# Second expert layer, phase 2: the transposes of a pair of token tiles rank ahead of the products of the pair before

## The chip, the core and the metric

The kernel runs on one core of one Trainium2 chip. The metric is the time of one execution on the device in microseconds (us), the median over several runs. The engines are PE (TensorE: matrix products and transposes), ACT (ScalarE), DVE (VectorE), POOL (GpSimd) and SP (SyncE, which here issues the DMAs). Each has its own stream of instructions and executes it in order; between engines there are semaphores.

## The reference

The reference has three stages, all in fp32. Attention with softmax over 4 batches, 12 heads, 448 positions and 64 channels, with a mixing of the heads before and after the softmax, gives 1792 tokens of 768 channels. A first expert layer takes them through a 2048 wide layer and a gate. The second expert layer, which the change touches, is

```
h    = x @ w_in                                   # 1792 x 1024
e    = exp(h - max(h));  sm = e / (sum(e) + 1e-9)
solu = h * sm
mu   = mean(solu);  var = mean((solu - mu)**2)
ln   = (solu - mu) / sqrt(var + 1e-6) * g_ln
out  = ln @ w_out                                 # 1792 x 768
```

## The kernel before

The second expert layer has two phases. Phase 1 computes h, phase 2 computes ln @ w_out. Each works on 7 pairs of 128-token tiles (14 tiles, numbered 0 to 13; pair p holds tiles 2p and 2p+1). A pair's matrix product is a 2 by 2 block product done in seven block products instead of eight; so a pair has seven *products*, numbered 0 to 6. In what follows [p,i] is product i of pair p in phase 2. A product of phase 2 is one call of `wide_mm` with 12 matmuls (L1184 to L1186, 128x384 each): four slices of the inner length, and for each the three partial products of values split into a high and a low part. A product of phase 1 is 9 matmuls of 128x512 on the same lines. g_ln is multiplied into the weights beforehand.

For phase 2 a tile goes through this chain. After phase 1 its exponentials, and for tiles 6 to 13 its h too, were written to DRAM. `el_load` (L1101) issues from SP the loads that bring them back: `el` are the exponentials, `hl` is h, 512 KB each. For pairs 3 to 6 there follows the chain `solu`: a sum and a reciprocal of small columns, `h2_solu` (L1145, DVE), `h2_mean` (L1150, POOL), `h2_square` (L1153, ACT), `h2_rstd` (L1156 to L1158, POOL). For pairs 0 to 2 that was done in phase 1. Then `el_ln` (L1169, ACT) normalises the tile in place, and `tr` (L1106, PE) transposes it: two calls per tile, i = 0 and 1, each four 128x128 transposes into one of 4 PSUM banks of the ring `pstr`. I write tr[t,i] for such a call. Of the transposed blocks, ACT makes plain copies (`lf_copy`, L1113), DVE sums of blocks (`l_sum`, L1119), and of each block or sum ACT makes the high part (`l_h`, L1130) and DVE the low part (`l_l`, L1133). These are the left operands of the products. A product accumulates in a PSUM bank; `part_copy` (L1201, ACT) and `part_add` (L1204, DVE) fold the banks into the output tile, and SP stores it (L1264).

The order of all this is written by a planner, the class `Order` (L69 to L191), while the kernel is built. Each task has an engine, a planned duration, a priority (a lower number goes first), the tasks that it needs, and places in rings of buffers. The planner plays the time through: on the engine that comes free first it takes, among the tasks that are ready by then in its plan, the one with the lowest priority number. What comes out is one fixed stream per engine; on the chip, an instruction waits for its semaphores at the head of its stream and holds up all behind it. The pairs' priorities are 20 apart: `make_front(p, q0)` makes the front of pair p (loads, solu, normalising, transposes) with numbers counted from q0, which is the number at which that pair's seven products start (q0 to q0 + 0.6). So the products of the pair before start at q0 - 20.

Of the kernel before, what the change touches and what calls it, by code (L numbers as in the profile page):

```python
# [68 lines left out]
class Order:  # L69
# [12 lines left out]
    def add(self, eng, dur, prio, fn, *a, deps=(), new=(), join=(), use=(), lat=None):  # L82
        dur = int(dur * SCALE.get(fn.__name__, 1))
        t = Task(eng, dur, (fn, a), prio, deps, lat)
        self.tasks.append(t)
        for r in new:
            r.first.append([t])
            r.users.append([t])
        for r in join:
            r.first[-1].append(t)  # L90
            r.users[-1].append(t)
        for r, k in use:
            r.users[k].append(t)
        return t
# [563 lines left out]
def moe(nc, od, pl, c1, c2, last_x, r_sr, r_psa, r_psb, near, xs, c_near, c_in2, c_out2, c_t1, c_t2, c_o2, xe2, xh2, w_in, w_out, w_in2, w_out2, g_ln, ident_in, out):  # L658
    add = od.add
# [3 lines left out]
    ring = {n: od.ring(b) for n, b in dict(raw=2, m=2, v=1, win=3, wout=3, xl=2, g=4, t=2, st2=3).items()}  # L663
# [220 lines left out]
    for s in range(NS):  # L884
# [20 lines left out]
        if 0 < s < NS - 1:  # L905
            for q in range(min(len(todo), 4 if s < 3 else 3)):
                e, pr = todo.pop(0), base - 6 + 10 * q
                if isinstance(e, tuple):
                    kk, i = e
# [4 lines left out]
        for ch in range(4):  # L914
# [3 lines left out]
            for i, j in enumerate(js):  # L918
                step, a = 1 if u < 2 else 6, None
                for k0 in range(0, 6, step):  # L920
                    a = add("PE", 567 * step, pr + i, h_mm, u, j, xk, k0, step, deps=[a] if a else wd['in', j] + xd[ch],
                            use=[(ring['win'], j), xi[ch]],
                            **(dict(join=[ring['psh']]) if a else dict(new=[ring['psh']])))
# [7 lines left out]
            for m in range(6):  # L931
                a = add("PE", 1134, pr + 14 + 0.1 * m, o_mm, u, js, m, deps=gs + wd['out', js[0]] + wd['out', js[1]] + [o2],
                        new=[ring['pso2']],
                        use=[(ring['wout'], js[0]), (ring['wout'], js[1]), (ring['g'], 2 * u), (ring['g'], 2 * u + 1)])
                b = add(*(("Activation", 424) if s == 0 else ("DVE", 531)), pr + (14 if u < 30 else -25) + 0.1 * m, o_add, u, s, ch, m,
                        deps=[a] + acc_d.get((ch, m), []), use=[(ring['pso2'], -1)])
# [52 lines left out]
    for k in range(3):  # L989
        for c in range(2):  # L990
            pr = 1285 + 2 * k + c
            r = (ring['raw'], len(ring['raw'].users))
            a = od.dma("SP", 900, 1500, pr - 8, prep1_load, k, c, new=[ring['raw']],
                       deps=[o1] + ([ready2[k + 3 * i, h] for i in range(2) for h in range(2)] if wide else []))
            a = add("DVE", 4 * 330, pr, prep1, k, c, deps=[a], use=[r])
# [65 lines left out]
    for i, (_, _, b) in enumerate(SEVEN):  # L1061
        for k in range(3):
            q, r = divmod(3 * i + k, 5)
            rg = ('sr', 'sr', 'xl', 'xl', 'w1x')[q]
            if b[0] == 'T':
                src, deps = c_t1[:, k, TI[b]], [t1_d[k, c] for c in range(2)]
            else:
                kk, h = k + 3 * (int(b[0]) - 1), int(b[1]) - 1
                src, deps = src_in2[:, kk, 512 * h:512 * h + 512], ([ready2[kk, h]] if wide else [])
# [90 lines left out]
    def solu(t, pr, deps, ue, uh):  # L1160
        x = add("Pool", 250, pr, h2_guard, t, deps=deps)
        x = add("DVE", 163, pr, h2_recip, t, deps=[x])
        y = add("DVE", 1360, pr, h2_solu, t, deps=[x], use=uh + ue)
        x = add("Pool", 250, pr, h2_mean, t, deps=[y])
        x = add("Activation", 1330, pr, h2_square, t, deps=[x], use=uh + ue)
        return y, add("Pool", 1300, pr, h2_rstd, t, deps=[x])
# [101 lines left out]
    for k in range(4):  # L1268
        pr = PR + 10 + 20 * k
        at, bs = len(ring['ot'].users), []  # L1270
        for i in range(2):
            a = od.dma("SP", 450, 1130, pr - 8, prep2_load, k, i, new=[ring['ot']], deps=[ch_, o2] + ([ready2[k + 4 * i]] if wide else []))
            a = add("Activation", 734, pr, prep2_gain, k, i, deps=[a], use=[(ring['ot'], -1)])
            t2_d[k, i, 0] = od.dma("SP", 450, 1130, pr, prep2_keep, k, i, deps=[a], use=[(ring['ot'], -1)])
            bs += [a, t2_d[k, i, 0]]
        a = add("Pool", 4 * 930, pr, prep2, k, deps=bs, use=[(ring['ot'], at), (ring['ot'], at + 1)])
# [7 lines left out]
    def make_front(p, q0):  # L1284
        for a in range(2):
            t = 2 * p + a
            rg = ring['h2' if p < EARLY else 'wout']
            ue, uh = [(rg, len(rg.users))], [(ring['h2'], len(ring['h2'].users))]
            x = od.dma("SP", 450, 1500, q0 - 25, el_load, t, 0, deps=[ln_d[t]], new=[rg])
            if p >= EARLY:  # L1290
                y = od.dma("SP", 450, 1500, q0 - 25, el_load, t, 1, deps=[lh_d[t]], new=[ring['h2']])
                _, x = solu(t, q0 - 11, [x, y, ls_d[t]], ue, uh)
            x = add("Activation", 1240, q0 - 11, el_ln, t, deps=[x, ls_d[t]], use=ue)
            for i in range(2):
                m = add("PE", 436, q0 - 12 + 0.1 * (2 * a + i), tr, t, i, deps=[x], new=[ring['pstr']], use=ue)
                front[t, i] = m, [(ring['pstr'], len(ring['pstr'].users) - 1)]

    for p in range(7):
        pr = PR + 20 * p
        if p == 6:  # L1300
            make_front(0, PR + 112)
# [4 lines left out]
        for dst, a, b, op_ in (('S1', '21', '22', ALU.add), ('S2', 'S1', '11', ALU.subtract), ('S3', '11', '21', ALU.subtract), ('S4', '12', 'S2', ALU.subtract)):  # L1306
# [3 lines left out]
                          use=[(ring['s'], si[q]) for q in (a, b) if q in si and q != dst])  # L1310
        ld = []
        for i, (_, q, _) in enumerate(SEVEN):
            us = [(ring['s'], si[q])] if q in si else []
            x = add("Activation", 500, px + 0.1 * i, x2_h, p, i, q, deps=[sm[q]] if q in sm else ad, use=us, new=[r_x2[i]])
# [6 lines left out]
        for a, (own, ds) in enumerate(seven(0, p, pr, ld, [sum((w1_d[i, k] for k in range(3)), []) for i in range(7)], r_x2)):  # L1321
            t = 2 * p + a
# [3 lines left out]
            ue = [(ring['wout'], -1)]  # L1326
# [19 lines left out]
    for p in range(7):  # L1346
        pr = PR + 300 + 20 * p
        if p:
            make_front(p, pr)
        lc, prev, q0 = {}, [], pr - (0, 168)[p == 0]  # L1350
        for a in range(2):
            for i in range(2):
                t = 2 * p + a
                q = '%d%d' % (a + 1, i + 1)
                m, up = front[t, i]
# [10 lines left out]
        for i, (_, q, _) in enumerate(SEVEN):  # L1366
# [7 lines left out]
            x = add("Activation", 595, q0 - 9 + 0.1 * i, l_h, p, i, q, use=us, new=[rl], deps=dep + before)  # L1374
            y = add("DVE", 675, q0 - 9 + 0.1 * i, l_l, p, i, q, deps=[x], use=us + [(rl, -1)])
            ld.append([x, y])
        for a, (own, ds) in enumerate(seven(1, p, pr, ld, [sum((w2_d[i, k] for k in range(4)), []) for i in range(7)], r_lt[p % 2])):
            t = 2 * p + a
# [83 lines left out]
```

## Time and profile before

| quantity | value |
|---|---|
| time, median of 3 runs | 1074.84 us (1074.3 to 1077.52) |
| time of the profiled execution | 1078.25 us |
| its span in the profile | 1076.4 us |
| mean granted TensorE clock over the span | 0.987 |
| PE busy | 1026.5 us, 95% of the span |
| DVE, ACT, POOL busy | 69%, 58%, 33% of the span |

The span is the time from the first to the last instruction that the profiler recorded; the execution's time holds 1.85 us more. PE is busy nearly throughout, so the time of the kernel is the PE's work plus what PE waits and what it loses to a lower clock. The granted clock is a share of full speed: 1.00 is the level of 2.4 GHz, and one half is the level of 1.2 GHz. Phase 2's products of pairs 1 to 6 run from 970 us on and end at 1073 us.

### The profile page before, as it was taken

What the parts mean: (1) busy time and instruction counts of PE and PEld (TensorE: products, weight loads), DVE (VectorE), ACT (ScalarE), POOL (GpSimd) and SP (SyncE); (2) the same over time, 40 slices, a digit from 0 to 9 for tenths busy, and PEclk for the clock granted to TensorE, in tenths of its full rate; (3) what the DMA queues carried; (4) which work ended last, traced back from release to release, by engine and by line L of the source; (5) the groups of instructions that cost most, each with busy time, mean ns of one, the idle gap of its engine ahead of it and who ended that gap; (6) DMA issues with size and microseconds to landing.
All of it is one profiled execution on the core that took longest, in us unless ns stands there. A gap on an engine that the chain in (4) does not pass through costs nothing.

```text
span 1076.4 us, 27349 instructions
## 1 busy us (share of the span) xinstructions
PE 1026.5 (95%) x11053; PEld 840.0 (78%) x11053; DVE 741.8 (69%) x1259; ACT 621.6 (58%) x1329; POOL 352.5 (33%) x475
## 2 busy tenths in 40 slices
PE   7779988999999899999999999999999999989998
PEld 2436555665666589999999999999999888889997
DVE  4445654555555863488898668898876999867674
ACT  3666967778878665533344344343435577767562
POOL 3111321211111341445555455554611244052110
PEclk9899999999999999999999999999999999998999
DMA  8766787478575560242424233423274556695321
GB/s 170 201 174 167 209 251 200 139 213 227 170 222 189 176 201 1 83 135 85 148 69 138 88 118 98 152 89 132 96 227 155 198 210 232 226 355 177 106 84 59
DMA packets 101422, 171.41 MB, mean 159 GB/s; under 512 B 22752, under 2 KB 77888, under 8 KB 101296
## 3 DMA queue, kind: packets, MB, share of 16 engines
q1 hardware_dynamic: 100560, 168.46, 50.3%
q0 software_dynamic: 736, 1.21, 0.6%
q8 instruction: 87, 1.43, 0.6%
q14 instruction: 39, 0.32, 0.1%
HBM read 91.07 MB, written 39.85 MB: 122 GB/s over the span
## 4 chain that ended last, share of the span: by engine, by line
PE 77%; DMA 11%; DVE 5%; ACT 4%; issue 2%; POOL 1%; SPq 1%; ACTq 0%; DVEq 0%
PE ps_h L820 7%; PE ps_o L850 7%; PE ps_h L822 7%; PE ps_o L852 7%; PE ps_h L821 7%; PE ps_o L851 7%; DMA sr<-s 5%; PE ps_pre L340 5%; PE ps_av L427 5%; PE ps_post L376 4%; PE ps_qk L313 4%; PE ps_h L1184 3%; PE ps_h L1186 3%; PE ps_h L1185 3%; PE ps_ot L1186 3%; PE ps_ot L1184 3%
## 5 line engine op out<-in xcount | busy, mean ns | idle before, releaser
L345 DVE TENSOR_REDUCE nm<-ps_pre 128x1 f32<-128x448 f32 x180 | 105.8, 618 | 54.1 <-PE ps_pre L340 45.0
L850 PE MATMUL ps_o<-g,wout 128*128 128x448 f32 x384 | 139.4, 363 | 0.3 <-DVE x2acc L860 0.3
L852 PE MATMUL ps_o<-g,wout 128*128 128x448 f32 x384 | 139.2, 363 | 0.0
L851 PE MATMUL ps_o<-g,wout 128*128 128x448 f32 x384 | 138.3, 360 | 0.0
L376 PEld LDWEIGHTS ps_post<-wr,p 64*64 64x64 f32 x5040 | 103.1, 135 | 43.9 <-issue 28.5
L350 ACT ACTIVATE p<-ps_pre,nm 128x448 f32<-128x448 f32 x180 | 114.1, 642 | 23.6 <-DVE nm L345 22.9
L313 PE MATMUL ps_qk<-kraw,qb 64*64 64x448 f32 (+2 forms) x768 | 110.2, 593 | 12.5 <-DMA qb<-in_q_dram 5.1
L842 POOL TENSOR_TENSOR g<-t,g 128x448 fp32r<-128x448 f32 x64 | 83.2, 1301 | 107.8 <-ACT g L838 106.8
L324 ACT ACTIVATE s<-ps_qk 119x448 f32<-119x448 f32 (+1 forms) x186 | 92.2, 567 | 41.8 <-PE ps_qk L313 30.2
L340 PE MATMUL ps_pre<-sr,wp 64*64 64x448 f32 (+1 forms) x720 | 104.3, 575 | 11.9 <-DMA vv<-in_v_dram 3.1
L860 DVE TENSOR_TENSOR x2acc<-ps_o,x2acc 128x448 f32<-128x448 f32 x168 | 100.3, 617 | 19.9 <-PE ps_o L852 18.6
L739 POOL TENSOR_TENSOR m<-m,v 128x768 f32<-128x768 f32 (+1 forms) x48 | 88.5, 1844 | 71.3 <-DVE v L721 56.3
L376 PE MATMUL ps_post<-wr,p 64*64 64x60 f32 x5040 | 104.4, 220 | 7.1 <-issue 3.7
L357 POOL TENSOR_SCALAR nm<-nm 128x2 f32<-128x2 f32 x90 | 19.5, 216 | 236.2 <-ACT p L350 236.1
L826 ACT ACTIVATE t<-ps_h,st 128x448 f32<-128x448 f32 x64 | 40.3, 630 | 69.1 <-PE ps_h L822 67.7
L711 ACT ACTIVATE v<-v,st 128x768 int32<-128x768 int32 (+1 forms) x48 | 42.2, 880 | 64.3 <-DVE v L707 64.1
L852 PEld LDWEIGHTS ps_o<-g,wout 128*128 128x128 f32 x384 | 72.1, 188 | 5.4
L851 PEld LDWEIGHTS ps_o<-g,wout 128*128 128x128 f32 x384 | 71.8, 187 | 5.2
L850 PEld LDWEIGHTS ps_o<-g,wout 128*128 128x128 f32 x384 | 72.0, 188 | 4.6 <-DVE x2acc L860 0.7
L340 PEld LDWEIGHTS ps_pre<-sr,wp 64*64 64x64 f32 (+1 forms) x720 | 30.4, 135 | 56.0 <-issue 17.3
L427 PE MATMUL ps_av<-at,vv 128*64 128x240 f32 (+1 forms) x648 | 70.0, 359 | 2.3 <-issue 2.3
L820 PE MATMUL ps_h<-sr,win 128*128 128x448 f32 x192 | 70.3, 366 | 0.0
(192 smaller groups left out, 2441.8 us busy)
## 6 DMA issues: line engine op xcount, KB each, us to landing
sr<-s SPq DMA_DIRECT2D x138, 192.5 KB
raw<-in_moe_w_out_dram SPq DMA_DIRECT2D x22, 768.0 KB
raw<-in_moe_w_in_dram SPq DMA_DIRECT2D x14, 768.0 KB
sr<-s SPq DMA_DIRECT2D x48, 210.0 KB
xe<-e SPq DMA_DIRECT2D x14, 512.0 KB
el<-xe SPq DMA_DIRECT2D x14, 512.0 KB
raw<-in_moe_w_in_dram SPq DMA_DIRECT2D x12, 512.0 KB
kraw<-in_k_dram SPq DMA_DIRECT2D x24, 224.0 KB
```

Of the source, the lines that this page charges most:

```text
L313: nc.tensor.matmul(out=qk_t[b, c, 2 * p + e][64 * j:at_], lhsT=qb[rows, i % 2, lo:hi], rhs=kraw_t[b, p][rows], start=True, stop=True,)
L324: nc.scalar.activation(out=s[:n], in_=qk_t.pop((b, c, h))[:n], func=AF.Copy, scale=0.125)
L340: nc.tensor.matmul(out=pre_t[t][o:o + 64], lhsT=wp[k_], rhs=sr[i % 2][k_, g, :], start=True, stop=True)
L345: nc.vector.tensor_reduce(nm_t[t // 2][:, 0, t % 2:t % 2 + 1], pre_t[t], axis=AX.X, op=ALU.max, negate=True)
L350: nc.scalar.activation(out=p, in_=pre_t.pop(t), func=AF.Exp, bias=nm[:, 0, e], accum_out=nm[:, 1, e])
L376: nc.tensor.matmul(out=ps[i][64 * j:64 * j + 64, k, :], lhsT=ps_p[e][64 * i:64 * i + 64, x:x + 64], rhs=wr[64 * i:64 * i + 64, e], start=T ...
L427: nc.tensor.matmul(out=ps[0][64 * j:64 * j + 64, a, :2 * w].rearrange("p (e s c) -> p e s c", e=2, c=SEG), lhsT=v_t[b][:, 1 + m, h * D:(h ...
L820: nc.tensor.matmul(out=ps, lhsT=wh, rhs=xh, start=(kk == 0), stop=False)
L850: nc.tensor.matmul(out=ps, lhsT=wh, rhs=g[:, 0], start=(i == 0), stop=False)
L851: nc.tensor.matmul(out=ps, lhsT=wh, rhs=g[:, 1], start=False, stop=False)
L852: nc.tensor.matmul(out=ps, lhsT=wl, rhs=g[:, 0], start=False, stop=(i == 1))
L860: nc.vector.tensor_tensor(out=dst, in0=op.pop((u, m)), in1=dst, op=ALU.add)
```

## The change

One number in `make_front` changes: the priority of the transposes goes from q0 - 12 to q0 - 20.5 (plus 0.1 per call in both). The loads keep q0 - 25, the solu chain and `el_ln` keep q0 - 11. Since the products of the pair before start at q0 - 20, a transposing call that is ready in the plan now goes ahead of the products of the pair before and no longer behind them.

```diff
@@ -1292,7 +1292,7 @@
                 _, x = solu(t, q0 - 11, [x, y, ls_d[t]], ue, uh)
             x = add("Activation", 1240, q0 - 11, el_ln, t, deps=[x, ls_d[t]], use=ue)
             for i in range(2):
-                m = add("PE", 436, q0 - 12 + 0.1 * (2 * a + i), tr, t, i, deps=[x], new=[ring['pstr']], use=ue)
+                m = add("PE", 436, q0 - 20.5 + 0.1 * (2 * a + i), tr, t, i, deps=[x], new=[ring['pstr']], use=ue)
                 front[t, i] = m, [(ring['pstr'], len(ring['pstr'].users) - 1)]
```

No instruction is added or taken away on PE; but since the planner plays the whole kernel through again, the streams of all engines change from about the middle of phase 1 on.

PE, at the change from pair 0 to pair 1. The rows on L1184 to L1186 that read `xl,x` are the last matmuls of product [0,6], those that read `acc_11232,xl` are product [1,0]. Before, all four calls of pair 1 (tr[3,0], tr[3,1], tr[2,0], tr[2,1]) stand there in one row, directly ahead of the first product that needs them:

```order
L1185 MATMUL ps_ot<-xl,x_10669 128x384
L1186 MATMUL ps_ot<-xl,x_10669 128x384
L1106 MATMUL ps_tr<-ident,el 128x128 x16
L1184 MATMUL ps_ot<-acc_11232,xl 128x384
L1185 MATMUL ps_ot<-acc_11232,xl 128x384
L1186 MATMUL ps_ot<-acc_11232,xl 128x384
```

Now the calls of tile 2 stand ahead of product [0,6] (the row of 8, with [0,6] behind it), and between [0,6] and [1,0] there is one call of pair 2, tr[4,0]:

```order
L1106 MATMUL ps_tr<-ident,el 128x128 x8
L1184 MATMUL ps_ot<-xl,x_10669 128x384
L1185 MATMUL ps_ot<-xl,x_10669 128x384
L1186 MATMUL ps_ot<-xl,x_10669 128x384
L1184 MATMUL ps_ot<-xl,x_10669 128x384
L1185 MATMUL ps_ot<-xl,x_10669 128x384
L1186 MATMUL ps_ot<-xl,x_10669 128x384
L1184 MATMUL ps_ot<-xl,x_10669 128x384
L1185 MATMUL ps_ot<-xl,x_10669 128x384
L1186 MATMUL ps_ot<-xl,x_10669 128x384
L1184 MATMUL ps_ot<-xl,x_10669 128x384
L1185 MATMUL ps_ot<-xl,x_10669 128x384
```

The calls of tile 3 have gone further forward, into pair 0 and the end of phase 1. Behind [1,0] there now follow tr[4,1], [2,0], tr[5,0], tr[5,1], [1,2], [1,1], [1,3], [1,4], [1,5], [1,6], tr[6,0], tr[6,1], [2,1], tr[7,0], tr[7,1], [2,2] to [2,6]. From pair 3 on, two or four calls of the next pair stand ahead of or among the products of a pair, and the products of pairs 3 to 6 stand in their natural order 0 to 6.

ACT, at the same place. Before, `el_11681` is tile 2 and `el_11835` is tile 5; `ps_tr_11869` and `ps_tr_11874` are the two halves of tile 2, and `xl_10608` from `ps_tr_11869` is the high part that product [1,0] reads:

```order
L1201 ACTIVATE ot_11775<-ps_ot_11645 128x384
L1169 ACTIVATE el_11681<-el_11681,st_6010 128x1024
L1130 ACTIVATE x2_10669<-ps_tr_11860 128x512
L1169 ACTIVATE el_11835<-el_11835,st_6010 128x1024
L1113 ACTIVATE lf_11883<-ps_tr_11869 128x512
L1130 ACTIVATE xl_10608<-ps_tr_11869 128x512
L1113 ACTIVATE lf_11886<-ps_tr_11874 128x512
L1130 ACTIVATE xl_10608<-ps_tr_11874 128x512
```

Now `el_11674` is tile 2, `el_11850` is tile 5, `ps_tr_11852` and `ps_tr_11858` are the halves of tile 2, `ps_tr_11642` and `ps_tr_11739` those of tile 3, and `ps_tr_11887` is tr[4,0]:

```order
L1169 ACTIVATE el_11674<-el_11674,st_6010 128x1024
L1113 ACTIVATE lf_11863<-ps_tr_11852 128x512
L1130 ACTIVATE xl_10608<-ps_tr_11852 128x512
L1113 ACTIVATE lf_11881<-ps_tr_11858 128x512
L1130 ACTIVATE xl_10608<-ps_tr_11858 128x512
L1113 ACTIVATE lf_11892<-ps_tr_11642 128x512
L1130 ACTIVATE acc2_11579<-ps_tr_11887 128x512
L1113 ACTIVATE lf_11911<-ps_tr_11739 128x512
L1169 ACTIVATE el_11850<-el_11850,st_6010 128x1024
L1201 ACTIVATE ot_11935<-ps_ot_11895 128x384
```

The normalising of tile 5 has moved from ahead of the high part for product [1,0] to behind seven copies, among them that high part.

SP, at the end of phase 1. Before, three loads of exponentials stand in a row (`el_11820`, `el_11835`, `el_11850`; the second is tile 5), and the loads of h of tiles 8 and 7 come behind two stores of outputs:

```order
L1043 DMA xl_10492<-c_t2_62 128x384 x4
L1261 DMA xh2_65<-h2_11664 128x1024
L1261 DMA xe2_64<-e_11749 128x1024
L1261 DMA xh2_65<-h2_11594 128x1024
L1261 DMA xe2_64<-e_11771 128x1024
L1101 DMA hl_11811<-xh2_65 128x1024
L1101 DMA el_11820<-xe2_64 128x1024
L1101 DMA el_11835<-xe2_64 128x1024
L1101 DMA el_11850<-xe2_64 128x1024
L1264 DMA out_0_dram<-ot_11775 128x768
```

Now a load of h of tile 8, `hl_11758`, stands ahead of the last four writes to DRAM; the load of tile 5 is `el_11850`, which now takes a buffer that tile 2 held, so that it can't start before the transposes of tile 2:

```order
L1043 DMA xl_10492<-c_t2_62 128x384 x4
L1101 DMA hl_11758<-xh2_65 128x1024
L1261 DMA xh2_65<-h2_11666 128x1024
L1261 DMA xe2_64<-e_11765 128x1024
L1261 DMA xh2_65<-h2_11594 128x1024
L1261 DMA xe2_64<-e_11787 128x1024
L1101 DMA hl_11829<-xh2_65 128x1024
L1101 DMA el_11848<-xe2_64 128x1024
L1101 DMA el_11850<-xe2_64 128x1024
L1264 DMA out_0_dram<-ot_11803 128x768
```

The load of tile 5 keeps its place behind the write of `e` and two other loads, but what it waits for has changed.

## Rows read from the trace of the kernel before

**Rows 1.** The page: its first line, the span.

```profile
span 1076.4 us, 27349 instructions
```

**Rows 2.** Windows: us; busy PE, PEld, DVE, ACT, POOL; granted clock, DMA share, GB/s.

```profile
950.00:963.00 13.00, 13.00 (x75) 12.77 (x74) 10.97 (x15) 7.74 (x15) 8.84 (x9) 1.00 1.01 364
963.00:970.00 7.00, 2.40 (x20) 2.13 (x18) 1.25 (x2) 2.67 (x4) 0.00 (x0) 0.89 0.97 353
970.00:980.00 10.00, 9.81 (x49) 9.45 (x50) 7.80 (x13) 7.56 (x16) 1.81 (x5) 0.74 0.47 153
...
1027.00:1032.00 5.00, 4.22 (x28) 3.91 (x27) 4.93 (x10) 4.92 (x10) 0.00 (x0) 1.00 0.49 155
```

**Rows 3.** PE in order of time: start, us, line, output<-inputs, [idle before <-releaser].

```profile
963.49 1.91 PE L1106 MATMUL ps_tr<-ident,el 128*128 128x128 f32 x16
970.19 0.69 PE L1184 MATMUL ps_ot<-acc,xl 128*128 128x384 f32 x1 [4.79 <-ACT xl L1130]
...
974.29 1.50 PE L1106 MATMUL ps_tr<-ident,el 128*128 128x128 f32 x8
975.54 0.43 PE L1184 MATMUL ps_ot<-sr,xl 128*128 128x384 f32 x1
```

**Rows 4.** ACT in order of time, 958 to 970 us.

```profile
958.81 1.23 ACT L1169 ACTIVATE el<-el,st 128x1024 f32<-128x1024 f32 x1
...
967.93 1.24 ACT L1169 ACTIVATE el<-el,st 128x1024 f32<-128x1024 f32 x1 [2.77 <-DMA el<-xe]
969.08 0.58 ACT L1113 ACTIVATE lf<-ps_tr 128x512 f32<-128x512 f32 x1
969.55 0.59 ACT L1130 ACTIVATE xl<-ps_tr 128x512 fp32r<-128x512 f32 x1
```

**Rows 5.** SP, 961.5 to 962.6 us: the load of tile 5.

```profile
961.82 0.32 SPq L1101 DMA_DIRECT2D el<-xe  x1
```

**Rows 6.** PE in order of time around the later waits.

```profile
1027.76 0.44 PE L1184 MATMUL ps_ot<-sr,acc 128*128 128x384 f32 x1
...
1029.14 0.44 PE L1186 MATMUL ps_ot<-sr,acc 128*128 128x384 f32 x1 [0.78 <-DVE acc L1133]
...
1031.01 0.34 PE L1184 MATMUL ps_ot<-acc,acc 128*128 128x384 f32 x1
...
1053.99 1.91 PE L1106 MATMUL ps_tr<-ident,el 128*128 128x128 f32 x16
1055.76 0.44 PE L1184 MATMUL ps_ot<-acc,acc 128*128 128x384 f32 x1
...
1059.07 0.44 PE L1184 MATMUL ps_ot<-sr,acc 128*128 128x384 f32 x1 [0.58 <-ACT ot L1201]
...
1067.63 0.34 PE L1184 MATMUL ps_ot<-sr,acc 128*128 128x384 f32 x1
...
1070.57 0.45 PE L1184 MATMUL ps_ot<-xl,x 128*128 128x384 f32 x1 [0.65 <-DVE ot L1204]
```

**Rows 7.** SP in order of time: start and time of issue.

```profile
951.89 0.65 SPq L1261 DMA_DIRECT2D xh<-h  x1
...
959.25 0.32 SPq L1101 DMA_DIRECT2D hl<-xh  x1
```

**Rows 8.** Lines, 942 to 1077 us: count, busy us, mean ns of one, idle before.

```profile
L1169 ACT ACTIVATE el<-el,st 128x1024 f32<-128x1024 f32 x11 | 13.7, 1243 | 9.9 <-POOL st L1158 7.1 <-DMA el<-xe 2.8
...
L1145 DVE SCALAR_TENSOR_TENSOR el<-hl,st,el 128x1024 f32<-128x1024 f32 x8 | 10.2, 1280 | 0.0
...
L1153 ACT ACTIVATE hl<-el,st 128x1024 f32<-128x1024 f32 x8 | 9.2, 1146 | 4.0 <-POOL st L1150 4.0
...
L1157 POOL TENSOR_TENSOR st<-st,mhalf 128x1 f32<-128x1 f32 x8 | 5.3, 656 | 0.7
```

**Rows 9.** SP in order of time: the load of tile 9.

```profile
1002.72 3.29 SPq L1101 DMA_DIRECT2D el<-xe  x2
```

**Rows 10.** PE in order of time: the transposes of tile 9.

```profile
1023.10 1.03 PE L1106 MATMUL ps_tr<-ident,el 128*128 128x128 f32 x8
```

## The prediction

> **What bounds the kernel now.** I read the page first, for the span; then windows over phase 2, to find where PE is not full; then PE in order of time at those places; and last ACT and SP in order of time, to see why PE waited there. The span is 1076.4 us [rows 1] and the execution took 1078.25, so 1.85 us lie outside the span. In 950 to 963 us PE is busy for all 13.00 us [rows 2]. Then comes a hole: in 963 to 970 us PE is busy for 2.40 of 7.00 us, and in 970 to 980 it is busy, but at a granted clock of 0.74 [rows 2].
>
> The hole is a wait of 4.79 us, ended by ACT's high part `xl` [rows 3]. ACT in order of time shows why that came late: at 967.93 us ACT normalises a tile, after 2.77 us of idle that a DMA ended, and only behind it come the copy and, at 969.55, the high part [rows 4]. By the order this normalising is tile 5's, which no product needs before pair 2, while the copies behind it are of tile 2, normalised by 958.81 + 1.23 = 960.04 [rows 4]. The load of tile 5 was issued at 961.82 [rows 5] and landed by 967.93, 6.1 us later, with the DMA engines full (shares of 1.01 and 0.97) [rows 2]. So PE waits for a load that it doesn't need yet: the transposes of pair 1 came so late that their copies stood behind that load on ACT.
>
> Three shorter waits follow in phase 2: 0.78 us at 1029.14 for DVE's low part, 0.58 at 1059.07 for ACT's `part_copy`, 0.65 at 1070.57 for DVE's `part_add` [rows 6].
>
> **What these cost PE, by the starts of instructions.** The measure of a product at full clock is the stretch from 1031.01 to 1053.99, which holds 11 products and nothing else: 22.98 / 11 = 2.09 us each. The measure of the transposes is the row of 16 at 1053.99 with its follower at 1055.76: 1.77 us, 0.44 per call [rows 6].
> - The wait: 970.19 - 963.49 - 1.77 = 4.93 us [rows 3].
> - The slow clock behind it: product [1,0] takes 974.29 - 970.19 = 4.10, which is 2.01 more than 2.09; the next two calls take 975.54 - 974.29 = 1.25, 0.37 more than 0.88 [rows 3].
> - The three later places: 3.25, 3.31 and 2.94 us where a product takes 2.09, so 1.16 + 1.22 + 0.85 = 3.23 too many [rows 6]. (The part of it that is not idle in the rows is that the first matmuls behind a wait are spread.)
>
> Together 4.93 + 2.01 + 0.37 + 3.23 = 10.54 us, 7.31 of them at the first place. More than this a better order can't take in phase 2, since the products themselves stay.
>
> **The change part by part.** On PE nothing is added or removed: the same transposes, 0.44 us per call, stand elsewhere.
>
> *What goes.* The high part of tile 2 now stands ahead of tile 5's normalising on ACT, and tile 2's calls a whole product ahead of [1,0]. Tile 3's two calls have moved into earlier, full stretches, so at 963.49 - 2.09 + 0.88 = 962.3 us [rows 3] PE starts tile 2's calls and ends them at 963.15. Copy and high part take 0.6 us each [rows 4] and are done by about 964.4; [0,6] runs to 965.24 and tr[4,0] to 965.68. So [1,0] finds its operand, and 4.93 goes; with the wait the slow clock behind it goes, 2.38. The three later waits go too. The one at 1029 stands right behind four calls of the next pair, with DVE's low parts queued in a heap; the new order spreads the calls. Those at 1059 and 1070 come from the last pair running its products in the order 0, 2, 3, 1, 5, 4, 6: product 2 stands right behind product 0 and waits until its bank has been copied out, and 6 right behind 4. In the natural order another product, 2.09 us, stands between in both places. I take all 10.54; the lower bound, if the later waits only move, is 7.31.
>
> *What is late next: tile 5.* Its load now takes the buffer that tile 2 held, so it can't start before tr[2,1] ends at about 963.15; I take 963.3, 1.5 us later than the 961.82 of before [rows 5]. How long it takes has no row in the new order. The nearest is its own 6.1 us; the longest such way in this stretch is from the write of h issued at 951.89 to the load that waited for it, 959.25, 7.4 us [rows 7]. Below, 512 KB at 364 GB/s [rows 2] are 1.44 us. I take the row of the same load: landed at 963.3 + 6.1 = 969.4. Normalising 1.24 [rows 4] and 0.2 for handing over give 970.85 for tr[5,0]. PE gets there at 965.68 + 2.09 ([1,0]) + 0.44 (tr[4,1]) + 2.09 ([2,0]) = 970.3. A new wait of 0.55 us, between 0 and 1.9.
>
> Behind it on ACT stand `part_copy` and the high parts of pair 1's sums, so [1,1] may miss its low part by about 0.15. The calls of tile 7 wait for a normalising that stands behind copies of tile 6: 0.3, between 0 and 1.4 (one more normalising in between, 1.24, and a hand-over).
>
> *What has cover.* The loads and the solu chain of pairs 3 to 6 now have to be done earlier than before, because the transposes stand earlier. The chain is 1.28 on DVE, 1.15 on ACT, 0.66 on POOL and 1.24 on ACT [rows 8], 4.3 us together, and with the longest load of 7.4 about 12 us. For tile 9 there were 1023.10 - 1002.72 = 20.4 us from the issue of the loads to its transposes [rows 9, 10]. In the new order ten products and four calls, 10 x 2.09 + 4 x 0.44 = 22.7 us, stand between the calls that set its buffer free and its own, so cover remains, and I cost it at nothing. If that cover is gone, rival D prices it. The load of h that SP now issues ahead of four writes of phase 1 delays these by one transfer of 1.44 us; what reads them back is again the load of tile 5 and its neighbours, inside the bound of 1.9.
>
> *Sum.* New waits 0.55 + 0.15 + 0.3 = 1.0. The span falls by 10.54 - 1.0 = 9.5 us, to 1066.9, and the profiled execution to 1068.75. That execution lies 3.41 us above the median of the runs, 1074.84. Against the median: 1074.84 - 9.5 = 1065.3 us.
>
> **A rule that speaks against it.** The rows show the clock at 1.00 in 1027 to 1032 us, with a wait of 0.78 in it, and below full only behind the wait of 4.79 [rows 2, 3, 6]. So short waits cost their own length here. The Trainium skill ("TensorE: Matmul & The Clock Gate", section "A second HAM failure mode: psum-queue depth-cycling") tells of short idles between groups of matmuls that made the clock swing between its two levels, with a loss each time. The trace does not bear this out at 0.6 to 0.8 us; rival E says what it would cost.
>
> **The rivals.**
> - A, the forecast: own range 1063 to 1068, from 0 to 3.3 us of new waits (1.9 + 1.4) around the 10.54.
> - B, tile 5 is late in earnest. With 7.4 us and another 1.44 for the load put ahead of it, it lands at 972.1, tr[5,0] starts at 973.6, and PE waits 3.3 us; a wait so long is likely to bring the slow clock again, 2.38. The gain is 10.54 - 3.3 - 2.38 - 0.45 = 4.4: 1070.4 us. For it: the DMA engines are full until 970 [rows 2]. Against: in 970 to 980 their share is 0.47, so the crowd is ending.
> - C, the hole moves rather than goes: tile 5 and tile 7 are both late like that, 2 x 3.3 + 2.38 = 9 us, and only about 1.4 us is gained: 1073.4, no change that can be told. Against: the load of tile 7 comes when the DMA engines are half idle.
> - D, slower: transposes at the head of PE's stream wait while products that are ready stand behind them. Before, a late tile cost nothing, as its calls stood last; now each of the pairs 3 to 6 puts calls ahead of products of the pair before. It needs more than 9.5 / 4 = 2.4 us of wait per pair to lose, as against 4.93 at the one place in the trace where the front was late. At 3.5 us per pair: 14 - 9.5 = 4.5 slower, 1079.3. Against: the 20.4 us of tile 9 [rows 9, 10].
> - E, short waits slow the clock: each of the three new ones costs 2.38 more, 7.1 together: 1072.4. Against: the 1.00 above.
>
> **How the numbers follow.** A 0.64, B 0.18, C 0.07, D 0.08, E 0.03. The measurement can tell about 0.3%, 3.2 us, from no change; that is 1071.6 to 1078.1. A and B lie below it; C and E mostly inside, and of D about a third. So faster 0.82, same 0.12, slower 0.06. The range goes from 1062.5, where everything goes and no new wait comes (1064.3) less the spread of runs, to 1071.5, so that it holds A and B, 0.82.
>
> **What would show it.** Right: PE busy in 963 to 970 us, clock near 1.00 in 970 to 980, [1,0] at 965.7, a short wait ahead of tr[5,0] near 970.5, the last products at a pitch of 2.09 and PE's end at about 1063.5. Wrong: a wait of over 3 us ahead of any `ps_tr` row that POOL's or a DMA's work to `el_ln` ended, above all at tiles 5, 7 or 8; or the waits for `part_copy` and `part_add` still there in the last pair.

## The result and the profile after

| | before | after |
|---|---|---|
| median of 12 runs each | 1074.94 us (1068.62 to 1082.39) | 1065.14 us (1057.08 to 1081.78) |
| span of the profiled execution | 1076.4 us | 1064.1 us |
| second expert layer on PE, first matmul to last | 843.85 to 1072.93: 229.08 us | 841.49 to 1060.64: 219.15 us |

The ratio of the times is 0.9885, 95% interval 0.9855 to 0.9916; the forecast was 1065.3 us. The ratio leaves out as slow those executions that took over 1.5% longer than the fastest of their kernel, five of the twelve after and none of the twelve before, so it shows a larger gain than the quotient of the medians, 0.9909. The third line is the better measure of what the change does: the streams are the same up to the second expert layer, and the time that the stages ahead of it take differs from one execution to the next (below). In the second layer itself the change takes 229.08 - 219.15 = 9.93 us off; the other 2.36 us between the two spans lie ahead of it and aren't the change's.

The windows after, with the columns of [rows 2]:

```profile
950.00:963.00 13.00, 12.68 (x75) 12.15 (x74) 10.64 (x16) 8.85 (x18) 5.89 (x7) 1.00 1.03 378
963.00:970.00 7.00, 7.00 (x47) 6.65 (x46) 4.30 (x7) 4.43 (x9) 0.00 (x0) 1.00 0.92 309
970.00:980.00 10.00, 9.98 (x58) 9.64 (x57) 10.00 (x20) 7.93 (x15) 2.15 (x6) 1.00 0.50 179
1027.00:1032.00 5.00, 5.00 (x37) 4.96 (x36) 2.66 (x5) 3.17 (x6) 0.86 (x2) 1.00 0.39 152
```

The hole of 963 to 970 us is gone: PE is busy for 7.00 us instead of 2.40, and in 970 to 980 the clock is 1.00 instead of 0.74, with the DMA engines nearly as full as before in 963 to 970 (0.92 against 0.97) [rows 2]. The waits of PE over phase 2 after (engine, line, what it waited for: us in total, times, longest; waits under 0.15 us are not listed) are a single one:

```profile
PE ps_ot L1184 <- ACT xl L1046: 0.3, 1, 0.3
```

So the three later waits [rows 6] have gone as well. The one that is left, 0.32 us at 955.99, is new: a product of pair 0 waits there for a piece of weights that ACT prepares (L1046). At pair 1, PE in order of time now reads so, where before there were the 16 transposes in one row and the wait [rows 3]:

```profile
960.42 1.03 PE L1106 MATMUL ps_tr<-ident,el 128*128 128x128 f32 x8
961.21 0.42 PE L1184 MATMUL ps_ot<-xl,x 128*128 128x384 f32 x1
...
963.73 0.42 PE L1184 MATMUL ps_ot<-acc,xl 128*128 128x384 f32 x1
...
968.56 1.09 PE L1106 MATMUL ps_tr<-ident,el 128*128 128x128 f32 x8
```

Tile 2's calls, product [0,6], [1,0] at 963.73 with no wait ahead of it, and at 968.56 tile 5's calls. How near tile 5 came is shown by ACT in order of time, which answers to [rows 4]:

```profile
961.54 0.59 ACT L1130 ACTIVATE xl<-ps_tr 128x512 fp32r<-128x512 f32 x1
...
967.27 1.24 ACT L1169 ACTIVATE el<-el,st 128x1024 f32<-128x1024 f32 x1 [2.17 <-DMA el<-xe]
```

and by SP, which answers to [rows 5]:

```profile
961.52 0.32 SPq L1101 DMA_DIRECT2D el<-xe  x1
```

The load of tile 5 still makes ACT wait, 2.17 us, but the high part for [1,0] now stands ahead of it, at 961.54, and nothing that PE needs soon stands behind it. Issued at 961.52 and landed at 967.27, the load took 5.75 us; the normalising ends at 968.51 and PE takes up tile 5 at 968.56. So PE did wait for it, some 0.1 us: from the last matmul of [2,0], which starts at 968.27, to tile 5's calls are 0.29 us, and the same step from a product to a transpose takes 0.18 us at 963.38.

### The profile page after: what moved, and what is told of

It is laid out like the page before. It is cut to its first block, busy times and chain, and to the rows that moved or that the text cites. A ratio compares the mean times of both kernels' runs of the same rounds, so it can differ in the third digit from the quotient of the medians.

```text
span 1064.1 us, 27355 instructions
## 1 busy us (share of the span) xinstructions
PE 1016.8 (96%) x11053; PEld 836.5 (79%) x11053; DVE 740.7 (70%) x1259; ACT 621.7 (58%) x1329; POOL 352.1 (33%) x475
## 4 chain that ended last, share of the span: by engine, by line
PE 80%; DMA 10%; DVE 4%; ACT 3%; issue 1%; SPq 1%; POOL 1%; ACTq 0%; DVEq 0%
PE ps_h L820 7%; PE ps_o L850 7%; PE ps_h L822 7%; PE ps_o L852 7%; PE ps_h L821 7%; PE ps_o L851 7%; PE ps_pre L340 6%; PE ps_post L376 5%; PE ps_av L427 4%; PE ps_qk L313 4%; DMA sr<-s 4%; PE ps_ot L1184 3%; PE ps_ot L1186 3%; PE ps_ot L1185 3%; PE ps_h L1184 3%; PE ps_h L1186 3%
## 5 line engine op out<-in xcount | busy, mean ns | idle before, releaser
L313 PE MATMUL ps_qk<-kraw,qb 64*64 64x448 f32 (+2 forms) x768 | 102.8, 568 | 15.1 <-DMA qb<-in_q_dram 5.8
L427 PE MATMUL ps_av<-at,vv 128*64 128x240 f32 (+1 forms) x648 | 68.3, 353 | 1.5 <-issue 1.5
```

What stands on the lines that cost most here:

```text
L313: nc.tensor.matmul(out=qk_t[b, c, 2 * p + e][64 * j:at_], lhsT=qb[rows, i % 2, lo:hi], rhs=kraw_t[b, p][rows], start=True, stop=True,)
L427: nc.tensor.matmul(out=ps[0][64 * j:64 * j + 64, a, :2 * w].rearrange("p (e s c) -> p e s c", e=2, c=SEG), lhsT=v_t[b][:, 1 + m, h * D:(h ...
```

## The experiments

All are measured by the stretch of the second expert layer on PE, first matmul to last, in one profile each; the ratio of times with its interval stands beside it.

**Pair 1 alone.** `q0 - 20.5` only where p == 1, `q0 - 12` elsewhere.

```diff
-  q0 - 12 + 0.1 * (2 * a + i), tr
+  q0 - (20.5 if p == 1 else 12) + 0.1 * (2 * a + i), tr
```

> Only the transposes of pair 1 get the new priority; those of the other pairs keep the old one. Measure: the stretch from the first matmul of the second expert layer to the end of the last one, 229.1 us before and 219.2 after the whole change. Theory (the first hole is 4.93 of wait and 2.38 of slow clock, and the waits of the last pair are the transposes of later pairs): the hole and its slow clock go, the waits near the last pair (0.58 and 0.65) stay, so about 229.1 - 7.3 = 221.8. Rival 1 (the gain comes from the order of the later pairs): 226 or more. Rival 2 (moving one pair's front only shifts the hole to the next pair): a wait of over 3 us ahead of a product of pair 1 or 2, and 226 or more.

Measured: 842.21 to 1063.47, 221.26 us; ratio 0.9919 (0.9880 to 0.9958). PE's waits in phase 2:

```profile
PE ps_tr L1106 <- ACT el L1169: 1.1, 1, 1.1
PE ps_ot L1184 <- DVE ot L1204: 0.7, 1, 0.7
PE ps_ot L1184 <- ACT ot L1201: 0.6, 1, 0.6
```

The hole is gone and the two waits of the last pair, 0.58 and 0.65 us, are still there to the hundredth [rows 6]. A wait for tile 5 of 1.06 us is new. Both rivals fall: 7.8 of the 9.9 us come with pair 1. The wait of 0.78 us for DVE's low part has gone too, though no pair but pair 1 has a new priority. The planner wrote the later streams anew, and the same product still stands right behind four calls in one row:

```profile
1018.15 1.91 PE L1106 MATMUL ps_tr<-ident,el 128*128 128x128 f32 x16
1019.82 0.42 PE L1184 MATMUL ps_ot<-sr,acc 128*128 128x384 f32 x1
```

What differs is that two products now stand between that row and the transposes ahead of it (the row of 8 at 1013.08), where before there was one (the row of 8 at 1023.10 [rows 10] and the next four calls at 1026.09).

**Pairs 2 to 6 alone.** The same line with `20.5 if p > 1 else 12`.

> Only the transposes of pairs 2 to 6 get the new priority; those of pair 1 keep the old one. In this order tile 5 is still normalised ahead of the high part that product [1,0] reads, and the products of pairs 3 to 6 stand in their natural order. Theory: the hole of pair 1 with its slow clock stays (7.3), the three later places go (3.2), so the stretch of the second layer is about 229.1 - 3.2 = 225.9. Rival (the whole order counts, any front that is moved closes the hole): about 220.

Measured: 838.87 to 1064.57, 225.70 us; ratio 0.9957 (0.9913 to 1.0001). One wait of PE is left in phase 2, the hole:

```profile
PE ps_tr L1106 <- DVE xl L1133: 6.1, 1, 6.1
```

and behind it, in the second of these windows (columns as in [rows 2]), the slow clock:

```profile
957.00:966.00 9.00, 3.24 (x25) 2.97 (x23) 1.66 (x4) 3.24 (x6) 0.00 (x0) 0.80 0.93 337
966.00:970.00 4.00, 3.65 (x15) 3.65 (x16) 2.85 (x6) 2.11 (x5) 0.00 (x0) 0.59 0.36 149
```

PE now waits one step further on: tr[4,0] stands ahead of [1,0] in this order and waits for a low part that DVE makes from a transposed block. The later waits go (the stretch is 3.4 us shorter in all), the hole stays as long as pair 1's copies stand behind tile 5 on ACT.

**ACT's order alone.** The kernel before; in the plan, tile 5's normalising comes behind the high part that [1,0] reads.

```diff
-  el_ln, t, deps=[x, ls_d[t]], use=ue)
+  el_ln, t, deps=[x, ls_d[t], *([lh_x[1, 0]] if t == 5 else [])], use=ue)
...
+  lh_x[p, i] = x        # the l_h of pair p, operand i
```

> The kernel before with all its priorities; only tile 5's normalising on ACT is put behind the high part that product [1,0] reads. The transposes of pair 1 still stand directly ahead of [1,0]. Theory (the hole is ACT's queue standing behind a load): PE waits only for the copy and the high part, about 1 us, and the clock stays up: of 4.93 + 2.38 some 6.3 go, the stretch is about 222.8, give or take 1 for the later pairs. Rival (the late transposes themselves make the hole, so it has to stay as long as they stand there): a wait of over 4 us, 228 or more.

Measured: 841.03 to 1064.94, 223.91 us; ratio 0.9941 (0.9895 to 0.9987). The transposes of pair 1 still stand in one row ahead of [1,0]:

```profile
960.66 1.91 PE L1106 MATMUL ps_tr<-ident,el 128*128 128x128 f32 x16
963.36 0.45 PE L1184 MATMUL ps_ot<-acc,xl 128*128 128x384 f32 x1 [0.79 <-ACT xl L1130]
```

The wait shrinks from 4.79 to 0.79 us, and the clock in 965 to 970 us is 1.00. Up to the start of [1,0] the order of the instructions of PE, DVE, POOL and SP is that of before; only ACT's differs. So the hole was ACT's queue behind the load and not the lateness of the transposes as such. The total is 1.1 us more than expected. A part of that is known: the planner also wrote the last pairs anew, and a wait of 1.1 us for ACT's high part stands there in place of the 0.58 of before. Where the rest lies isn't shown.

**The last pair in natural order.** The kernel before; each product of pair 6 depends in the plan on the one ahead of it.

```diff
+  prev = [row[-1]] if ph and p == 6 and row else []
...
-  deps=deps + ldeps[i] + wdeps[i] + [co_]
+  deps=deps + ldeps[i] + wdeps[i] + [co_] + prev
```

> The kernel before; only the products of the last pair are put into their natural order 0 to 6, the transposes stay late. Theory (the natural order is only open to a pair whose transposes came early): product 1 of the pair needs a sum of blocks whose low part DVE finished starting at 1062.06 us before, and it would now stand at 1058; PE waits about 4 us and the clock falls behind it (2.4), against 2.1 us of the two waits that go: stretch about 229.1 + 4.3 = 233.4. Rival (the order of the last pair alone made those waits): about 227.0.

Measured: 836.75 to 1071.37, 234.62 us; ratio 1.0048 (0.9999 to 1.0098). The first three products of the last pair now start so, on PE in order of time:

```profile
1049.55 0.44 PE L1184 MATMUL ps_ot<-acc,acc 128*128 128x384 f32 x1
...
1055.44 0.69 PE L1184 MATMUL ps_ot<-acc,acc 128*128 128x384 f32 x1 [3.16 <-ACT acc L1130]
...
1059.94 0.53 PE L1184 MATMUL ps_ot<-sr,acc 128*128 128x384 f32 x1
```

and a window behind the wait has the clock at 0.50:

```profile
1056.00:1060.00 4.00, 3.87 (x13) 3.42 (x12) 1.73 (x3) 0.59 (x1) 0.00 (x0) 0.50 0.00 0
```

Product 1 waits 3.16 us for the high part of a sum of blocks and then runs at half the clock, 4.50 us instead of 2.09. By the starts before and after, the place costs 4.7 us more than with the old order; the rest of the 5.5 is a longer hole at pair 1 in that execution (5.5 us of wait). So in this kernel the natural order doesn't pay by itself: with late transposes the sums aren't made in time. The order of the last pair was a consequence of the late transposes.

**A number further out, same streams.** `q0 - 33`, with which the planner writes the same streams as with `q0 - 20.5`.

> The changed kernel with q0 - 33 in the place of q0 - 20.5. The planner writes the same five streams of instructions with both, so this is a second execution of the changed program: stretch of the second layer 219.2, give or take 0.5. Theory (the front of tile 5 comes only just in time, with 0.1 to 0.2 us to spare): from one execution to the next the wait ahead of tr[5,0] lies between 0 and 1.5 us, and no other wait is over 1 us. Rival (the first profile was lucky): a wait of over 3 us ahead of tr[5,0] or tr[7,0], with a clock below full behind it, stretch 223 or more.

Measured: 847.87 to 1066.67, 218.80 us, no wait but the one of 0.3 us; tile 5's load, issued at 968.00, was there by 972.57, after 4.57 us; it made ACT idle for 0.99 us only, and the normalising ended 1.1 us before PE came to the tile. The theory's 0.1 to 0.2 us to spare was too narrow: the first profile had none, this one 1.1 us. The ratio was 0.9974 (0.9926 to 1.0022): more on that below.

**Two pairs ahead.** `q0 - 45`.

> q0 - 45: transposes that are ready go ahead of the products of the two pairs before; the order differs from the changed kernel from product [1,6] on. Rival D of the prediction (transposes at the head of PE's stream wait while ready products stand behind them): waits of 2 us or more ahead of transposes of tiles 6 to 13, stretch 223 or more. Theory (the loads and the normalising have 20 us of cover, and four banks limit how far ahead transposes can go): no wait over 1 us, stretch 219 to 220.5.

Measured: 833.46 to 1053.38, 219.92 us; ratio 0.9965 (0.9925 to 1.0006). PE's waits:

```profile
PE ps_tr L1106 <- ACT el L1169: 0.4, 1, 0.4
PE ps_ot L1184 <- ACT xl L1046: 0.3, 1, 0.3
```

The first of them is for tile 5. Nothing waits at tiles 6 to 13. Rival D has no place here; nor is there anything more to gain.

**Tile 5's load made slower.** The changed kernel, with one more load of 512 KB into the same buffer ahead of the real one.

```diff
+  if t == 5 and not what:
+      nc.sync.dma_start(out=d, in_=xe2[:, 4])
```

> The changed kernel; into tile 5's buffer a second, useless load of 512 KB goes first (tile 4's values), and the real one after it; all results are the reference's. This is rival B of the prediction made real. If tile 5's front has no time to spare, the second load, some 2 to 4 us, comes out as a wait of PE ahead of tr[5,0] of 2 to 4 us; from there two answers: the clock falls behind that wait as it did behind the 4.79 us (another 1 to 2.4 us): stretch 222.5 to 225.5; or the clock stays at 1.00 as it did around the waits of 0.6 to 0.8: stretch 221 to 223. If there is more slack than the profile showed: 219.5 or less.

Measured: 840.24 to 1062.37, 222.13 us; ratio 0.9959 (0.9923 to 0.9996). The first load was issued at 960.46, the second at 964.66. PE at tile 5's calls:

```profile
970.30 1.09 PE L1108 MATMUL ps_tr<-ident,el 128*128 128x128 f32 x8 [2.75 <-ACT el L1171]
```

and the window behind them:

```profile
970.00:980.00 10.00, 9.69 (x57) 9.35 (x58) 8.82 (x17) 8.25 (x17) 1.72 (x5) 1.00 0.65 224
```

The second load was there by 969.00, and the delay comes out on PE as a wait of 2.75 us: what tile 5's front has to spare, between nothing and 1.1 us so far, doesn't cover one more load. The clock stayed at 1.00 behind it, so the loss is the wait (and some 0.3 us of spread matmuls) alone.

**Pairs 2 to 6 with ACT's order.** The edits of the second and the third run together.

> The new priority for pairs 2 to 6 only (as in the run of that name), and tile 5's normalising behind the high part for product [1,0] (as in the run on ACT alone). Pair 1's transposes stay directly ahead of [1,0]. Theory (the two gains are separate and add): of the hole of 7.3 all but a wait of 1.5 to 2 us goes (tr[4,0] now stands ahead of [1,0] and needs the bank that tile 2's copies and its low part free), the 3.2 of the later places go too: stretch of the second layer about 220.3. Rival (pair 1's transposes have to come early for the gain): 223 or more.

Measured: 834.14 to 1053.88, 219.74 us; ratio 0.9933 (0.9902 to 0.9964). One wait, 1.52 us ahead of tr[4,0]. The two parts add up to 9.3 us, 0.6 short of the whole change, with pair 1's transposes where they always were.

**The changed streams once more, and the kernel before once more.** `q0 - 25`, and the unchanged file.

> The changed kernel with q0 - 25, the same five streams once more, timed in more rounds. Stretch of the second layer 219, give or take 0.5. Theory (the gain is about 10 us in every execution, and what differs between timings comes from the stages ahead of it): the ratio of times comes out between 0.988 and 0.994, and the start of the second layer in the profile lies anywhere between 833 and 848 us. Rival (unprofiled runs gain less than the profiled one): 0.996 or more.

> The kernel before, once more, for a second profile of it. Theory (the hole is a property of the order, since tile 5's load takes about 6 us in every execution): stretch of the second layer 229.1, give or take 1; a wait of 4 to 6 us ahead of [1,0], the slow clock behind it, and the three later places of 1.2, 1.2 and 0.9. Rival (the profile of before was an unlucky one and the gain is smaller as a rule): 226 or less. The ratio of times is 1.000 within 0.005.

Measured: `q0 - 25`, 842.25 to 1061.31, 219.06 us, ratio 0.9939 (0.9906 to 0.9972). Before: 831.99 to 1060.93, 228.94 us, ratio 1.0023 (0.9977 to 1.0068). Its hole, which answers to [rows 3]:

```profile
951.90 1.91 PE L1106 MATMUL ps_tr<-ident,el 128*128 128x128 f32 x16
957.78 0.69 PE L1184 MATMUL ps_ot<-acc,xl 128*128 128x384 f32 x1 [3.98 <-ACT xl L1130]
...
961.87 1.91 PE L1106 MATMUL ps_tr<-ident,el 128*128 128x128 f32 x8
963.43 0.55 PE L1184 MATMUL ps_ot<-sr,xl 128*128 128x384 f32 x1
```

A wait of 3.98 us where the first profile had 4.79, a granted clock of 0.50 in 957 to 963 us, and the three later waits of 0.8, 0.6 and 0.7. The shorter wait costs hardly less: [1,0] takes 4.09 us against 4.10, but the two calls behind it take 963.43 - 961.87 = 1.56 us where the first profile had 1.25 [rows 3]. Before is 228.94 and 229.08, the changed streams 219.15, 218.80 and 219.06: the gain in this stretch is 10.0 us, and within either group the profiles lie 0.35 us apart at most.

## Why the prediction was right, step by step

- *The hole and its slow clock, 4.93 + 2.38.* Shown: it goes with pair 1 alone (221.26), stays with all other pairs (225.70), and shrinks to 0.79 us by ACT's order alone. That the queue on ACT was its cause is thereby shown.
- *The three later places, 3.23.* Shown in size: 3.4 us in the run with pairs 2 to 6. Of the two reasons that the prediction gave, neither held as it stood. For the place at 1029 it said that the wait stands right behind four calls in one row and that the new order spreads the calls. But the wait is gone with pair 1 alone, where the four calls still stand in that row, and the changed kernel too has rows of four with no wait behind them, this one among them:

```profile
1013.00 1.91 PE L1106 MATMUL ps_tr<-ident,el 128*128 128x128 f32 x16
1014.67 0.42 PE L1184 MATMUL ps_ot<-acc,acc 128*128 128x384 f32 x1
```

The rows fit the further product that stands there with pair 1 alone: DVE has 1019.82 - 1013.08 = 6.74 us from the row of 8 to the product, and had 1027.76 - 1023.10 = 4.66 [rows 6, 10]. That wasn't tried by itself. For the last pair it named the order of the products. That was half of the truth: the order by itself, forced without the early transposes, costs 4.7 us.
- *New waits, 1.0.* This was the term that was mis-sized. Tile 5 was costed at 0.55, [1,1] at 0.15 and tile 7 at 0.3; in three profiles of the changed streams none of them is listed as a wait, and by the starts only tile 5's 0.1 us of the first profile is there. Only the range from 0 holds. The load of tile 5 took 5.75, 4.57 and (with `q0 - 25`) 4.51 us, where the prediction took the 6.1 of [rows 5] for all; in the first profile it was issued 0.3 us behind the end of tile 2's calls, where 0.15 had been reckoned, and the hand-over from the normalising to PE, for which 0.2 was taken without a row, took 0.05. Instead, 0.32 us came at a place that the prediction did not look at, a piece of weights on ACT.
- *Sum.* 10.54 less that new place (0.5 by the starts: the matmul at 955.99 comes 0.66 us behind the one ahead of it, where 0.17 is the pitch) is 10.0, which is what the stretch shows; 9.5 was forecast.
- *Rivals.* B is real as a mechanism: one more load of 512 KB brings the wait of 2.75 us. It didn't occur by itself. Its second term, the slow clock, did not come with 2.75 us of wait; B's own wait was 3.3 us, and behind the 3.16 us of the run with the natural order it did come. C needs it twice and never showed. D found no place even two pairs ahead. E: short waits of 0.79, 1.06 and 1.52 us left the clock at 1.00. The Trainium skill ("TensorE: Matmul & The Clock Gate", section "A second HAM failure mode: psum-queue depth-cycling") tells of a clock that swings where PE idles shortly and often between groups of matmuls. Single waits of 0.79 to 1.52 us did not bring that here; many of them close together stand in no run.
- *The median.* 1065.14 against 1065.3 is closer than the method allows, and so luck. The same changed streams, timed three times, gave ratios of 0.9885, 0.9974 and 0.9939; 10.0 us of 1074.9 would be 0.9907, which lies in the first interval, at the edge of the last and just outside the second. Over all executions on record of these three timings the 34 of the changed streams have a mean of 1068.7 us and the 59 of before 1075.3: a gain of 6.7 us, give or take about 2.6. So the 10.0 us are shown for the second layer in the profiles; that the whole kernel gains as much as that is not shown. Where the scatter arises, the last section tells.

## What to carry to other kernels

When PE waits for a small copy, look at what stands ahead of that copy in its own engine's queue: an instruction that waits for a transfer which isn't urgent holds up all that is. An order can be fixed at either end, by producing the operand earlier or by moving the waiting instruction back, and the second is one dependency. Alone it gave 5.2 us here, the early transposes of pair 1 alone 7.8. Measure such a change over the stretch that it touches, from the profile, when the rest of the kernel varies by more than the change, and give the time of the whole kernel beside it.

## What the runs showed that was not expected

The stages ahead of the second layer, whose instructions were the same in all these kernels, ended anywhere between 831.99 and 847.87 us: a scatter of 16 us, while the second layer repeated within 0.4 us with the same streams. Between the two profiles of before all of it arises early in attention: the first matmul of L427 came at 87.23 us in the first profile of before and at 75.07 in the second:

```profile
87.23 2.65 PE L427 MATMUL ps_av<-at,vv 128*64 128x240 f32 x24
```

```profile
75.07 2.65 PE L427 MATMUL ps_av<-at,vv 128*64 128x240 f32 x24
```

Ahead of that matmul the first profile has a wait of PE of 4.30 us for a load of `kraw`, at 77.68 us, which the second has not. In other runs a part arises later: from that matmul to the first of the second layer it takes 756.0 us (`q0 - 45`) to 763.9 us (pairs 2 to 6 alone). Why was not tried. And of the clock: behind waits of PE of 0.79, 1.06, 1.52 and 2.75 us the rows show 1.00, behind those of 3.16, 3.98, 4.79, 5.5 and 6.11 us the matmuls ran at half speed for some 3 to 6 us (0.50 in the window of the run with the natural order). Whether the length of the wait alone decides that, no run here shows.
